# A new issue order for the first third of a two-layer state-space and local-attention kernel

## The chip, the cores and the metric

The kernel runs on one core of a Trainium2 chip. A core has a matrix engine (PE, fed by its weight loads, PEld), a vector engine (DVE), a scalar engine (ACT), a general engine (POOL) and a queue engine (SP) that issues DMAs; each takes its instructions in order from a queue of its own, and semaphores make one wait for another. The metric is the device time of one execution in microseconds. The kernel before takes 423.9 us, the median of three runs (423.18 to 425.21).

## The reference

The input u is 2048 tokens by 512 channels. Two layers follow each other, and the pair is applied twice with the same weights.

```python
x = A_u
x = x + A(layernorm(x))      # long convolution
x = x + B(layernorm(x))      # local attention, 32 heads, 8 keys at distance 0, 2, ... 14
x = x + A(layernorm(x))
x = x + B(layernorm(x))
# A: for each channel d a convolution kernel over 2048 lags l
logdA = dt * (A_re + 1j * A_im)
P = exp(logdA[:, :, None] * l)               # 512 channels x 128 modes x 2048 lags
K = einsum("dn,dnl,dn->dl", C, P, dt * B).real
y = irfft(rfft(u padded) * rfft(K padded))[:2048] + u * Dskip
```

K depends on the weights alone, so its spectrum is computed once and used by both A layers.

## The kernel before

The work falls into five stretches. From 0 to about 153 us the kernel builds the tables, the spectrum of K, the first stage of the Fourier transform of the normed input and the first convolution; the rest is attention, convolution, attention. Only the first stretch is touched.

**The order.** `KGEN` (line 353) is one string of words, and `run` (line 769) executes the words one after the other, each issuing a few instructions with a fixed engine. So the string sets the order of every engine's queue. A word may not stand ahead of the words whose results it needs; semaphores do the waiting on the chip. Where a copy can be done by two engines, the word's ending says which.

**The words.** K is handled in four quarters c = 0..3 of 128 channels.

- `q`, `m`, `l` (0 to 10) square the complex powers of exp(dt*A) eleven times: `q` squares on ACT, `m` and `l` combine on DVE; `b` copies a power to bf16 on ACT. `x0` to `x3` multiply C, dt and B on DVE, `x5` copies the result on ACT. `y` and `t` are a small copy and a load of an activation table.
- `U4:c`, `U2:c`, `U1:c`, `U256:c`, `U1024:c`, `U512:c` and `v2:c`, `v4:c`, `v8:c`, `v16..:c` extend the two tables U and V of quarter c by complex multiplication on DVE (lines 460 to 508). A name with `p` leaves the sums of products to PE: `+name` adds them by matmuls with the identity into PSUM (line 521), `=name` copies the result into the table on ACT (line 531); `0` or `1` behind the sign is the real or imaginary part. Without `p` the sums are `%name` on DVE (line 510). With `n` there are no sums, and a second table W takes the other products (line 483). `u:c`, `A:c`, `B:c` copy start columns into U and V; with `a` on ACT, else on DVE.
- `pcq` (line 558) is a product of U and V on PE, its four parts q = 0..3, in 34 matmuls, or 66 where W is used (`p00` to `p03`, `p12`, `p13`, `p20` to `p23`). `kc0` and `kc1` (line 575) copy two products each to SBUF on ACT; behind the second, four DMAs write them to DRAM (two on SP, two on POOL) and one DMA on POOL reads them back as `rows`. Since there are two tables U and two V, quarter c overwrites what quarter c - 2 has read.
- `sci` (line 593) multiplies `rows` of quarter c by a DFT matrix on PE, ten matmuls where all is done by PE (s01 to s03, s10 to s12) and five elsewhere; `oci` copies it on ACT, `eci` adds and subtracts on DVE, and the result is stored to DRAM in two DMAs on SP.
- `nj` and `Nj` (0 to 15) are statistics and application of the first layernorm, on DVE, or with `a` on ACT; `r0`, `r1`, `a0`, `a1` turn the statistics of eight rows each into scale and shift. `fj` (line 633) is the first DFT stage of row block j on PE, `zj` its copy out of PSUM, whole on ACT, or `a` and `v` for the real half on ACT and the imaginary one on DVE.
- `@Xg` words are the convolution of channel group g = 0..15: `T` transposes on PE, `t` or `a` copies (DVE or ACT), `X` second DFT stage on PE, `c` copy on ACT, `p` product with the spectrum on DVE, `v` inverse stage on PE, `V` copy on ACT (`W`: on DVE), `k` load of the spectrum for later groups by SP. Group 15 is done in halves, whose second parts are `d`, `q`, `i`, `I`. `U0` and `Y1` to `Y3` treat the last lag on DVE. After the last inverse stage PE begins the rows of y (`ps_y`, line 339).
- `w03:n` issues matmuls of n columns on PE that compute nothing used, into the PSUM tile that product or spectrum is going to take.

**PSUM.** The tiles of products and first stages (`psk`) and those of sums and spectra (`psg`) have two buffers each. A third waits until the first has been copied out.

The listing has the functions behind these words.

Of the kernel before, what the change touches and what calls it, by code (L numbers as in the profile page):

```python
# [1728 lines left out]
```

## Time and profile before

| What | us |
|---|---|
| median of three runs | 423.9 |
| lowest and highest | 423.18, 425.21 |
| the profiled execution | 424.25 |
| its span in the trace | 422.4 |
| DVE, PE, ACT busy in the span | 398.4, 379.3, 332.7 |
| POOL busy | 26.0 |
| DVE, ACT, PE busy from 0 to 160 us | 148.81, 145.33, 129.26 |

The page is one execution seen by the hardware profiler. A row of groups gives a line of the kernel, an engine, an operation with output and inputs, how often, its busy time, the mean duration of one, and the idle time of the engine ahead of it with what ended that. A row of the timeline gives the start, the time up to the end of the last merged instruction, the engine, the line and the tiles; in square brackets stands the idle time before it. One instruction's duration includes a part that overlaps with the next of its engine, so for a queue that never waits the spacing of starts is what counts. The ends of matmuls are modelled.

### The profile page before, as it was taken

How to read it: one execution, taken by the hardware profiler on the slowest of the kernel's cores; microseconds unless marked ns; L12 is line 12 of the kernel's file. 1: busy time of each engine (PE TensorE's matmuls, PEld its weight loads, DVE VectorE, ACT ScalarE, POOL GpSimd, SP SyncE). 2: the span in 40 equal slices, each digit the busy share in tenths (PEclk: the TensorE clock that was granted, in tenths of full speed). 3: DMA queues.
4: the chain of work that ended last, by engine and by line, in shares of the span. 5: the costliest groups of instructions: out<-in, count | busy, mean ns of one | idle time of the engine just before them, and what ended most of it. 6: DMA issues, size and time to landing. Idle time of an engine off the chain costs nothing.

```text
span 422.4 us, 12235 instructions
## 1 busy us (share of the span) xinstructions
PE 379.3 (90%) x5120; PEld 259.1 (61%) x5120; DVE 398.4 (94%) x730; ACT 332.7 (79%) x600; POOL 26.0 (6%) x68
## 2 busy tenths in 40 slices
PE   1157898999989999999999999889999999997996
PEld 1023585676458755587866575278855686875663
DVE  5999999999889979899999999999989999999994
ACT  6999998998979989766665699989988676663542
POOL 5000011001210000002020000000000001200000
PEclk9999999999999999999999999999999999998999
DMA  8900001254889960005480028239300009350022
GB/s 241 424 29 0 2 12 42 76 166 104 250 245 276 259 213 2 2 2 98 81 174 3 2 64 238 102 107 288 107 0 4 2 2 166 73 115 2 2 102 101
DMA packets 25822, 44.09 MB, mean 104 GB/s; under 512 B 7317, under 2 KB 17238, under 8 KB 25126
## 3 DMA queue, kind: packets, MB, share of 16 engines
q1 hardware_dynamic: 22918, 38.09, 31.9%
q0 software_dynamic: 1888, 4.56, 5.0%
q8 instruction: 40, 0.66, 0.6%
q10 hardware_dynamic: 960, 0.66, 0.5%
q14 instruction: 16, 0.13, 0.1%
HBM read 29.04 MB, written 6.95 MB: 85 GB/s over the span
## 4 chain that ended last, share of the span: by engine, by line
PE 46%; DVE 25%; ACT 7%; DMA 6%; issue 4%; SPq 2%; DVEq 0%; ACTq 0%
PE ps_qk L1207 10%; DVE prodpv L1403 9%; PE ps_v L1294 5%; DVE prodqk L1257 4%; PE vp L291 3%; PE psg L601 3%; PE Lp L1279 3%; PE po L1413 3%; PE ps_o L1443 2%; DVE Z L504 2%; DVE pab L275 2%; DMA Kt<-kt_scratch 2%; PE psk L568 2%; DMA V<-V 2%; ACT Z L1496 2%
## 5 line engine op out<-in xcount | busy, mean ns | idle before, releaser
L1403 DVE TENSOR_TENSOR prodpv<-V,Lsb 128x2048 bf16<-128x2048 bf16 x64 | 75.3, 1221 | 0.7 <-DMA V<-V 0.4
L1207 PE MATMUL ps_qk<-xnT,wqk 128*128 128x512 bf16 x256 | 59.9, 379 | 0.0
L1255 DVE TENSOR_TENSOR prodqk<-qT,N 128x1024 bf16<-128x1024 bf16 (+3 forms) x88 | 42.6, 544 | 1.9 <-ACT N L1210 1.9
L1257 DVE TENSOR_TENSOR prodqk<-qT,N 128x1024 bf16<-128x1024 bf16 (+3 forms) x56 | 40.4, 765 | 0.3 <-ACT qT L1210 0.2
L1413 PEld LDWEIGHTS <-prodpv 128*128 128x128 bf16 x1024 | 35.3, 100 | 7.2 <-DVE prodpv L1403 2.0
L275 DVE TENSOR_TENSOR pab<-xc,Kt 128x2048 bf16<-128x2048 bf16 (+1 forms) x34 | 38.8, 1154 | 0.7 <-issue 0.4
L1413 PE MATMUL po<-halves,prodpv 128*128 128x64 bf16 x1024 | 38.1, 196 | 0.9 <-DVE prodpv L1403 0.9
L1207 PEld LDWEIGHTS <-wqk 128*128 128x128 bf16 x256 | 23.7, 98 | 23.5
L269 ACT CAST xc<-xp 128x1024 bf16<-128x1024 f32 (+1 forms) x34 | 34.6, 1033 | 2.2 <-PE xp L263 1.9
L291 PEld LDWEIGHTS <-pab 128*128 128x128 bf16 x512 | 30.4, 98 | 7.0 <-DVE pab L275 3.5
L291 PE MATMUL vp<-sb_IC,pab 128*128 128x128 bf16 x512 | 33.6, 219 | 0.6 <-DVE pab L275 0.3
L1279 PEld LDWEIGHTS <-prodqk 128*128 128x128 bf16 x1024 | 29.8, 96 | 5.5 <-DVE prodqk L1257 2.5
L295 ACT CAST VT<-vp 128x1024 bf16<-128x1024 f32 (+1 forms) x31 | 32.7, 1065 | 0.6 <-PE vp L291 0.6
L1443 PE MATMUL ps_o<-wo_t,oT 128*128 128x512 bf16 x128 | 33.0, 379 | 0.0
L1279 PE MATMUL Lp<-sb_bones,prodqk 128*128 128x8 bf16 x1024 | 30.5, 166 | 1.0 <-DVE prodqk L1257 0.8
L528 PE MATMUL psadd<-Z,sb_ident 128*128 128x384 bf16 (+3 forms) x75 | 18.7, 337 | 13.1 <-DVE Z L504 7.9
L1294 PE MATMUL ps_v<-wv,xnT 128*128 128x256 bf16 x256 | 30.4, 272 | 0.0
L1424 ACT CAST oT<-po 128x512 bf16<-128x512 f32 x32 | 17.7, 589 | 13.8 <-PE po L1413 13.7
L1210 ACT CAST N<-ps_qk 128x512 bf16<-128x512 f32 x32 | 18.7, 587 | 12.1 <-PE ps_qk L1207 11.9
L1160 DVE BATCH_NORM_STATS2 ln_stats<-X 128x6 f32<-128x512 bf16 x39 | 24.9, 682 | 2.7 <-ACT X L1549 2.7
L1301 ACT CAST V<-ps_v 128x512 bf16<-128x512 f32 x32 | 18.2, 588 | 10.9 <-PE ps_v L1294 10.8
L1294 PEld LDWEIGHTS <-xnT 128*128 128x128 bf16 x256 | 24.2, 98 | 3.2
(202 smaller groups left out, 837.8 us busy)
## 6 DMA issues: line engine op xcount, KB each, us to landing
Kt<-kt_scratch SPq DMA_DIRECT2D x60, 256.0 KB, 5.5
kt_scratch<-ks SPq DMA_DIRECT2D x32, 128.0 KB, 3.0
G<-c_G SPq DMA_DIRECT2D x2, 1536.0 KB
V<-V SPq DMA_DIRECT2D x8, 288.0 KB, 7.8
X<-in_A_u_dram SPq DMA_DIRECT2D x4, 512.0 KB, 4.8
F1Tsb<-c_F1T SPq DMA_DIRECT2D x2, 1024.0 KB
V<-V SPq DMA_DIRECT2D x4, 512.0 KB
V<-V POOLq DMA_DIRECT2D x4, 384.0 KB, 8.3
```

The source lines that it names most:

```text
L269: nc.scalar.copy(xcs[cg][:, gs].rearrange("q g o l -> q (g o l)"), xps[cg][:].rearrange("q h n -> q (h n)")[:, gs.start * 128:gs.stop * 128])
L275: nc.vector.tensor_tensor(pabs[cg][:, gs], xcs[cg][:, gs].to_broadcast([128, gs.stop - gs.start, 2, 128]), kts[cg][:, gs], ALU.mult)
L291: a.last_pe = nc.tensor.matmul(vp[:, g, :], pabs[cg][:, gs.start + g, ab, :], C["IC"][:, ab, :], start=(ab == 0), stop=(ab == 1))
L295: copy(dst[..., parts(cg)[part]], vps.pop((cg, part))[:].rearrange("k g (q e) -> k q e g", e=GE))
L1207: nc.tensor.matmul(t.ps[:], wqk[:, ct, f0:f0 + 128], x_group(g)[:, :, ct], start=(ct == 0), stop=(ct == 3))
L1255: nc.vector.tensor_tensor(b.pr[:, u:u + 2 * n, 1 - halves_of[0], :], q, cols(kT[i][:, starts[0]:starts[0] + n * 128]), ALU.mult)
L1257: nc.vector.tensor_tensor(b.pr[:, u:u + 2 * n].rearrange("f u a q -> f a u q")[:, ::-1], q.unsqueeze(1).to_broadcast([128, 2, 2 * n, 64]), ...
L1279: nc.tensor.matmul(t.Lp[:, w, u % 2, u // 2, :], b.pr[:, u].rearrange("f a q -> f (a q)"), bones[:], start=False, stop=(t.parts == W // 2 ...
L1294: nc.tensor.matmul(t.ps[:, jj, :], tokens(ct, jp * 2 + jj, c), wv[:, ct, fp * 256:(fp + 1) * 256], start=(jj + ct == 0), stop=(jj == 1 and ...
L1403: nc.vector.tensor_tensor(t.p2[:, c:c + k, 0:nj, :].rearrange("p c j (d h) -> p c j d h", d=DH), m.V2[i // 2][:, c0 + c:c0 + c + k, r0:r0 ...
L1413: nc.tensor.matmul(po[jj // k][:, jj % k, c, :], t.p2[:, c - c0, jj, :], fold, start=(first and c == c0 and jj % k == 0), stop=(last and c ...
L1443: nc.tensor.matmul(t["ps"][:], m.oT[:, ft, j * 128:(j + 1) * 128], wo_t[:, ft, :], start=(start and ft == lo), stop=(ft == 3 or kept and f ...
```

## The change

The string `KGEN` is replaced by another that holds nearly the same words in another order. Some words change their engine. For the normed rows: n2 goes to ACT, n5 and n9 to DVE; N4, N11 and N12 go to ACT, N0, N5 and N15 to DVE. For the start columns: u:1 goes to ACT, B:1 to DVE. In the first DFT stage nine blocks are copied whole on ACT, five are split between ACT and DVE, and two are split with both halves on ACT; before, eight were whole and eight split. In the convolution V11 and V12 become W11 and W12 on DVE, W15 becomes V15 on ACT, and a4 with t3 take the place of a3 with t4.

The idle matmuls are written in another way: `~n` sets a number of columns, and the next PSUM tile that is taken by a sum, a product, a spectrum or a first stage gets them ahead of its own matmuls. There were 14,720 columns in twelve places, there are 8,576 in six. The words `kcm` get a variant on DVE, which the new order doesn't use.

```diff
-KGEN = ("m0 q0 b0 x1 l0 m1 q1 x0 t l1 b1 x3 x2 q2 m2 b2 l2 x5 m3 U4p:1 q3 U4:0 l3 b3 %U4:0 u:1 m4 q4 u:0 l4 b4 m5 q5 U2p:0 l5 +U2p:0 b5 "
...
-        "=0v8p:0 +U1024p:1 =1v8p:0 =U1024p:1 +U1024p:0 v8p:1 b9 +1v8p:1 w03:128 =U1024p:0 =1v8p:1 v16yn:0 +0v8p:1 w03:512 n5a U512:0 m10 "
-        "q10 %U512:0 n3a =0v8p:1 U512p:1 w03:6144 p03 n9a v16xn:0 p02 n14a +0U512p:1 +1U512p:1 v16x:1 n0a n2 =1U512p:1 l10 prep p00 n4a "
-        "k01 v16yn:1 =0U512p:1 p01 %v16x:1 v2:2 n1a U4p:2 Aa:2 %v2:2 p12 k00 c0 +U4p:2 ua:2 =U4p:2 v4p:2 Ba:2 U2:2 %U2:2 p13 +v4p:2 n6a "
-        "U256:2 k11 p10 =v4p:2 U1p:2 p11 w23:256 %U256:2 v2p:3 n7a +v2p:3 r0 =v2p:3 +U1p:2 Aa:3 v8p:2 =U1p:2 U1024:2 k10 U4:3 s01 ua:3 "
-        "%U1024:2 +1v8p:2 o01 v4:3 %U4:3 a0 =1v8p:2 +0v8p:2 %v4:3 U2p:3 n8a s03 =0v8p:2 c1 U512:2 +U2p:3 o03 =U2p:3 v16yn:2 n12a s02 "
...
-        "o10 k21 U512:3 p21 n13a %v8:3 N1a %U512:3 p20 n11a k20 v16x:3 s11 n10a %v16x:3 s13 o11 o13 p31 r1 v16y:3 N6a a1 p30 N0a %v16y:3 "
-        "k30 s00 N12 N13 f6 N8 N11 z6 p32 o00 e13 p33 N15a f1 k31 e00 z1a s23 z1v N10 f3 N14 o23 f12 N9 z3 z12v s20 z12a f11 o20 f5 e23 "
...
-        "@T12 @t12 @U0 @X10 @v8 @V7 @c10 @T13 @X11 @V8 @p10 @k15 @t13 @c11 @p11 @v9 @T14 @X12 @V9 @c12 @v10 @V10 @t14 @p12 @T15 @X13 @v11 "
-        "@c13 @X14 @V11 @t15 @c14 @p13 @p14 @v12 @V12 @X15 @c15 @d15 @p15 @q15 @v13 @v14 @v15 @i15 @Y1 @Y2 @V13 @V14 @W15 @Y3 @I15")
+KGEN = ("x0 q0 m0 l0 x2 t q1 b0 m1 l1 q2 b2 b1 x1 m2 l2 x3 q3 m3 l3 m4 x5 U4p:1 U4:0 +U4p:1 u:0 %U4:0 U2p:0 +U2p:0 b3 q4 b4 ua:1 =U4p:1 =U2p:0 "
+        "l4 v2p:0 v2:1 m5 U2p:1 U1p:0 +v2p:0 +U2p:1 q5 b5 =v2p:0 =U2p:1 l5 q6 n5 m6 l6 %v2:1 Aa:1 +U1p:0 y Aa:0 q7 =U1p:0 m7 v4p:1 l7 v4p:0 "
+        "U1p:1 b8 U256:1 b6 q8 ~2688 +v4p:1 ~1408 +v4p:0 m8 l8 b7 =v4p:0 =v4p:1 Ba:0 q9 U256p:0 ~128 +U256p:0 %U256:1 m9 B:1 l9 =U256p:0 +U1p:1 "
+        "b10 v8p:0 U1024p:1 U1024p:0 m10 =U1p:1 ~2432 +0v8p:0 n3a =0v8p:0 +1v8p:0 =1v8p:0 n9 +U1024p:0 b9 =U1024p:0 +U1024p:1 v8p:1 U512:0 q10 "
+        "=U1024p:1 l10 %U512:0 prep +0v8p:1 +1v8p:1 =0v8p:1 n14a =1v8p:1 n0a U512p:1 v16yn:0 v16xn:0 ~1152 p00 +1U512p:1 =1U512p:1 +0U512p:1 "
+        "=0U512p:1 n4a n2a n1a p03 p01 v16x:1 p02 ua:2 Aa:2 k00 v2:2 U4p:2 ~768 +U4p:2 %v2:2 %v16x:1 =U4p:2 v4p:2 U2:2 v16yn:1 %U2:2 c0 k01 s01 "
+        "o01 +v4p:2 p10 =v4p:2 n6a Ba:2 s03 n7a o03 n8a p11 p13 k10 U256:2 U1p:2 %U256:2 +U1p:2 p12 v2p:3 v8p:2 =U1p:2 +v2p:3 c1 =v2p:3 Aa:3 "
+        "ua:3 U1024:2 +0v8p:2 +1v8p:2 U4:3 %U1024:2 %U4:3 v4:3 U2p:3 k11 =0v8p:2 =1v8p:2 %v4:3 +U2p:3 s02 =U2p:3 U512:2 U256:3 %U512:2 %U256:3 "
+        "U1:3 U1024p:3 %U1:3 v16yn:2 c2 n12a s12 o02 r0 a0 Ba:3 o12 p23 +U1024p:3 n15a =U1024p:3 n13a s10 p22 s11 o10 n11a v8:3 U512:3 %v8:3 "
+        "%U512:3 v16xn:2 p20 s13 k21 N6a o11 s00 n10a r1 o13 N2a N3a o00 a1 v16x:3 v16y:3 %v16x:3 %v16y:3 N14 e13 N5 e00 N10 N8 N11a p21 p33 "
+        "N1a k20 p32 p30 p31 k31 N4a k30 N12a N7a f6 f11 z6 z11 f1 z1 s23 o23 e23 f5 z5 f3 z31a s20 o20 f8 z30v e20 z8 s21 o21 N0 f4 z4 f7 z70a "
+        "e21 s22 f14 s32 o22 z14 o32 N13 z71v f13 z13 f2 e22 z20v s33 z21a o33 e32 e33 f0 f10 z0 z100a s30 f12 o30 N9 N15 z101a z121v z120a s31 "
+        "o31 e30 f15 z150v f9 z91a z151a z90a @T0 @T1 @t0 @k4 @X0 @T2 e31 @t1 @c0 @T3 @t2 @p0 @t3 @X1 @c1 @k5 @p1 @T4 @v0 @X2 @a4 @c2 @T5 @V0 "
+        "@k6 @v1 @X3 @T6 @t5 @T7 @c3 @U0 @p2 @k7 @Y1 @p3 @X4 @V1 @v3 @c4 @X5 @v2 @k8 @V3 @c5 @V2 @t6 @p4 @t7 @T8 @p5 @t8 @X6 @c6 @v4 @V4 @k9 "
+        "@T9 @X7 @c7 @v5 @k10 @V5 @T10 @X8 @t9 @p6 @t10 @c8 @p7 @Y2 @p8 @v6 @T11 @V6 @k11 @X9 @v8 @T12 @c9 @X10 @v7 @V8 @c10 @V7 @k12 @k13 @t11 "
+        "@T13 @X11 @p9 @c11 @k14 @v9 @V9 @Y3 @t12 @T14 @X12 @p10 @v10 @c12 @V10 @t13 @T15 @p11 @t14 @t15 @p12 @X13 @c13 @p13 @v13 @V13 @k15 "
+        "@v11 @X14 @v12 @W11 @W12 @c14 @p14 @X15 @c15 @p15 @v15 @V15 @d15 @q15 @i15 @I15 @v14 @V14")
...
+        def fresh(tile):
+            warm(tile, late.pop("fill", 0))
+            return tile
...
-            ps = tiles["+", name, c, rs] = psum()[1].tile([128, 2, 512], F32, name="psadd", tag="psg")
+            ps = tiles["+", name, c, rs] = fresh(psum()[1].tile([128, 2, 512], F32, name="psadd", tag="psg"))
...
-            if part == "v":
-                nc.vector.tensor_copy(C["z_view"][:, 1, j], src[:, 1])
-            elif part == "a":
-                nc.scalar.copy(C["z_view"][:, 0, j], src[:, 0])
-            else:
+            if not part:
                 nc.scalar.copy(C["z_view"][:, :, j], src)
+                return
+            r = int(part[0])
+            (nc.scalar.copy if part[1] == "a" else nc.vector.tensor_copy)(C["z_view"][:, r, j], src[:, r])
...
-            if full[0] in "wW":
...
+            if full[0] == "~":
+                word(full, lambda full=full: late.update(fill=int(full[1:])))
```

More of the change, by code (lines that the diff above doesn't have):

```diff
@@ L508, in step, with warm @@
                 C["powers_used"] = last
+        def warm(tile, cols):
+            flat = tile[:].rearrange("n a b -> n (a b)")
+            while cols > 0:
+                n = min(cols, 512)
+                nc.tensor.matmul(flat[:, 0:n], C["ident"][:], C["ident"][:].unsqueeze(1).to_broadcast([128, n // 128, 128]), start=True, stop=True)
+                cols -= n
+        def fresh(tile):
+            warm(tile, late.pop("fill", 0))
+            return tile
         def sum_dve(name, c):
@@ L546, in spectrum_tile @@
             if ("s", c, i) not in tiles:
-                tiles["s", c, i] = psum()[1].tile([128, 2, 512], F32, name="psg", tag="psg")
+                tiles["s", c, i] = fresh(psum()[1].tile([128, 2, 512], F32, name="psg", tag="psg"))
             return tiles["s", c, i]
-        def warm(tile, cols):
-            flat = tile[:].rearrange("n a b -> n (a b)")
-            while cols > 0:
-                n = min(cols, 512)
-                nc.tensor.matmul(flat[:, 0:n], C["ident"][:], C["ident"][:].unsqueeze(1).to_broadcast([128, n // 128, 128]), start=True, stop=True)
-                cols -= n
         def product(c, q):
@@ L633, in first_stage @@
         def first_stage(j):
-            ps = tiles["f", j] = psum()[0].tile([128, 2, D], F32, name="ps_s1", tag="psk")
+            ps = tiles["f", j] = fresh(psum()[0].tile([128, 2, D], F32, name="ps_s1", tag="psk"))
             for r in range(2):
@@ L725, in kgen @@
             for m in range(2):
-                word(f"k{c}{m}", lambda c=c, m=m: product_out(c, m), f"p{c}{2 * m}", f"p{c}{2 * m + 1}", "prep")
+                for v, copy in (("", nc.scalar.copy), ("v", nc.vector.tensor_copy)):
+                    word(f"k{c}{m}{v}", lambda c=c, m=m, copy=copy: product_out(c, m, copy), f"p{c}{2 * m}", f"p{c}{2 * m + 1}", "prep")
             for i in range(4):
-                word(f"s{c}{i}", lambda c=c, i=i: spectrum(c, i), f"k{c}0", f"k{c}1")
+                word(f"s{c}{i}", lambda c=c, i=i: spectrum(c, i), *[w for w in everything if w.rstrip("v") in (f"k{c}0", f"k{c}1")])
                 word(f"o{c}{i}", lambda c=c, i=i: spectrum_odd(c, i), f"s{c}{i}")
```

9 lines of the change are left out of this document (4 added, 5 removed), and 8 rows, old and new, of the table KGEN.

## The prediction

> **What bounds the kernel now.** I read the page's busy times, then the 160 us of the changed stages (busy time, chain, waits), then the timeline of each engine there, and last the tiles and queues that a moved step touches.
>
> ```profile
> DVE  5999999999889979899999999999989999999994
> ```
> ```profile
> sum 160.00, PE 129.26 PEld 86.08 DVE 148.81 ACT 145.33 POOL 17.04; mean PE 8.08 PEld 5.38 DVE 9.30 ACT 9.08 POOL 1.06
> ```
> ```profile
> by line: PE psg L601 8.5%; DVE Z L504 6.5%; DMA Kt<-kt_scratch 6.4%; PE psk L568 6.3%; DVE pab L275 5.7%; issue 4.2%; PE psg L606 3.7%; DVE zt L254 2.5%; DVE Vsecond L483 2.2%; PE psadd L528 2.0%; DVE Vtab L483 1.9%; DMA kt_scratch<-ks 1.7%
> ```
> ```profile
> PE psadd L528 <- DVE Z L504: 8.3, 5, 6.4
> ...
> DVE Z L641 <- ACT Z L643: 2.6, 4, 1.2
> ```
>
> The first row is DVE's busy share in forty slices of the span, full from the second to the last. The sum row of the windows from 0 to 160 us: DVE works 148.8 us and ACT 145.3, so neither has room for a wait of more than a few us. The chain of these 160 us, by line, hops between all engines and the DMAs. The waits (total, places, longest) are long only on PE, which has time; DVE's longest is 2.6 us over four places. A new order has perhaps 5 us to win and everything to lose, and what counts is whether a queue gets blocked. Each engine takes its words in the written order, and that is how the timeline shows them: the products stand on PE in the list's order p03 p02 p00 p01 p12, and ACT's copies k01, k00 likewise.
>
> **The change part by part.** The anchors of the old order:
>
> ```profile
> 9.47 0.69 DVE L431 SCALAR_TENSOR_TENSOR lad<-lad 128x512 f32<-128x512 f32 x1
> ...
> 53.57 2.25 DVE L504 TENSOR_TENSOR Z<-Vtab,Z 128x1920 bf16<-128x1920 bf16 x2
> 55.71 0.72 DVE L179 BATCH_NORM_STATS2 n_stats<-X 128x6 f32<-128x512 bf16 x1
> ...
> 56.75 0.68 DVE L434 TENSOR_TENSOR L<-sq 128x512 bf16<-128x512 f32 x1
> 57.35 0.65 DVE L483 TENSOR_TENSOR Vtab<-Vtab,Z 128x960 bf16<-128x960 bf16 x1
> ...
> 61.84 0.69 DVE L663 TENSOR_TENSOR cl<-cb,L 128x1024 bf16<-128x1024 bf16 x1
> ...
> 98.80 1.38 DVE L204 TENSOR_SCALAR N<-X,n_rstd,n_nb 128x512 bf16<-128x512 bf16 x4
> ...
> 147.22 1.20 DVE L275 TENSOR_TENSOR pab<-xc,Kt 128x2048 bf16<-128x2048 bf16 x1
> ```
> ```profile
> 23.48 0.59 PE L528 MATMUL psadd<-Z,sb_ident 128*128 128x256 bf16 x2 [6.36 <-DVE Z L504]
> ...
> 24.72 1.48 PE L555 MATMUL psk<-sb_ident 128*128 128x512 bf16 x3
> 26.00 0.39 PE L528 MATMUL psadd<-Z,sb_ident 128*128 128x128 bf16 x2
> ...
> 53.40 0.50 PE L528 MATMUL psadd<-Z,sb_ident 128*128 128x512 bf16 x2
> ...
> 54.80 0.43 PE L568 MATMUL psk<-Utab,Vtab 128*64 128x40 bf16 x8
> ...
> 60.47 0.68 PE L568 MATMUL psk<-Utab,Vtab 128*64 128x40 bf16 x16
> ...
> 69.55 2.35 PE L601 MATMUL psg<-G,rows 128*128 128x512 bf16 x10
> 71.74 0.92 PE L528 MATMUL psadd<-Z,sb_ident 128*128 128x512 bf16 x4
> ...
> 96.06 0.43 PE L568 MATMUL psk<-Utab,Vtab 128*64 128x40 bf16 x8
> ...
> 98.22 1.27 PE L606 MATMUL psg<-G,rows 128*128 128x512 bf16 x5
> ...
> 119.53 0.68 PE L248 MATMUL pt<-sb_ident,Z 128*128 128x128 bf16 x9 [0.23 <-DVE Z L641]
> ...
> 152.18 0.35 PE L339 MATMUL ps_y<-VT,F1Tsb 128*128 128x448 bf16 x1
> ```
>
> A row of the timeline: start, us to its last end, engine, line, what. Costs are spacings from one start to the next. n on DVE: 55.71 to 56.75, 1.04. The two sums of U512p:1: 53.40 to 54.80, 1.4. Three products with the second table: 54.80 to 61.15, 2.1 each; two without: 96.06 to 98.22, 1.08 each. A whole spectrum: ten matmuls, 69.55 to 71.74, 2.2. v16xn:0 ended at 53.57, %v2:2 at 61.84, the tables at 98.80; the convolution's transposes began at 119.53, p13 ended at 148.4 and the rows of y began at 152.18.
>
> Step 1, p00 first. The new PE list is p00, +1U512p:1, +0U512p:1, p03, p01, p02, where the old one began with p03 p02 and both sums. p00 needs v16xn:0. DVE has more before that word: n5, n9 (2.08), l10 (0.60), B:1 (a 768-element copy, no row; between 0.2 and 0.6, I take 0.5 as a product of that width), less u:1 (0.15). So v16xn:0 ends at 53.57 + 3.03 = 56.6. p00's third and fourth blocks of matmuls need its last instruction: end 57.6. PE has had nothing to do for some 6 us since the sums of v8p:1, so its first matmuls run at half rate (three 512-column fills took 0.43 each from 24.72 to 26.00, after an idle of 6.4; the warm spacing is 0.22): I add 0.4. Then 1.4 of sums and 3 x 2.1: p02 ends at 65.75. DVE's v16x:1, v2:2, U4p:2 (2.96) are over at 59.6, and %v2:2 overwrites the table that p02 reads: done at 65.9, not 59.9. **Wait of 6.0 on DVE.** Behind the same sums ACT waits too, about as long (=1U512p:1).
>
> Step 2, s01 at once behind k01.
>
> ```profile
> 52.26 0.63 ACT L184 ACTIVATE n_junk<-X 128x512 bf16<-128x512 bf16 x1
> ...
> 53.87 0.63 ACT L184 ACTIVATE n_junk<-X 128x512 bf16<-128x512 bf16 x1
> ...
> 60.77 0.67 ACT L579 CAST KT<-psk 128x640 bf16<-128x640 f32 x1
> ...
> 62.34 0.90 ACT L697 COPY Vtab<-Z 128x768 bf16<-128x768 bf16 x1
> 63.12 0.63 ACT L184 ACTIVATE n_junk<-X 128x512 bf16<-128x512 bf16 x1
> ...
> 71.94 1.01 ACT L617 CAST ks<-psg 128x1024 bf16<-128x1024 f32 x1 [0.34 <-PE psg L601]
> 72.85 0.91 ACT L535 CAST Vtab<-psadd 128x896 bf16<-128x896 f32 x1
> ...
> 102.12 0.69 ACT L579 CAST KT<-psk 128x640 bf16<-128x640 f32 x1
> ```
> ```profile
> 66.61 0.77 POOL L590 DMA_DIRECT2D rows<-rows_scratch  x1 [3.74 <-DMA rows_scratch<-KT]
> ```
> ```profile
> 106.33 0.77 POOL L590 DMA_DIRECT2D rows<-rows_scratch  x1 [2.12 <-PE ps_s L636]
> ```
> ```profile
> DMA to landing us min/median/max: 2.7/3.0/3.2
> ```
>
> s01 reads rows that go through DRAM: after k00 and k01 there are two writes on SP, two on POOL, and a read on POOL that waits for them. In the old order the second copy ended at 61.44 and s01 began at 69.55: 8.1 us, in which PE did p12, p13, p10, p11 and three sums. The new PE queue has s01 right behind +U4p:2, and ahead of +v4p:2, p10, s03, p11, p13, +U1p:2, p12; ACT has o01 right behind k01, ahead of =v4p:2, n6a and Ba:2. After p02 ACT does ua:2 0.40, Aa:2 0.54, k00 0.58, =U4p:2 0.32, k01 0.58, with 0.1 for handing over: 68.3. Rows at 76.4 (the first trip's own 8.1; the last one took 6.5, from 102.81 to 106.33 plus the read's median of 3.0 in the last row). s01 takes 2.2 plus 1.2 for half rate after 10 us of idle: 79.8. Then o01 0.91 (71.94 to 72.85), =v4p:2 0.74, n6a 1.61 (52.26 to 53.87), Ba:2 0.78 (62.34 to 63.12): 83.9. DVE's ten words from %v16x:1 to v2p:3 are 9.6 us, done at 75.5; v8p:2 needs Ba:2. **Wait of 8.4 on DVE, about 11 on ACT.**
>
> The PE clock first by the row: half rate held for 2.5 us from 23.48, which prices s01 at +1.2. The Trainium skill, "TensorE: Matmul & The Clock Gate", Part 1, says that an idle window of about 3.4 us halves the clock and that a busy window of that length restores it; by it s01 would cost some 0.4 more and the sum would be 456. For the DRAM trip the rows say 8.1. The Trainium skill, "DMA: Bandwidth & Descriptors", on the fixed cost, gives about 2.0 us per DMA, an estimate of 4 for write and read; by that the sum would be about 451, and the trace's single read (2.7 to 3.2) does not agree.
>
> Step 3. PE's eight words behind s01, up to +v2p:3, are 10.4 us (s03 2.2, two long products 4.2, two short 2.2, three sums 1.8 by their columns at 0.22 per 512): 90.2. =v2p:3 and Aa:3 on ACT: 91.1. v4:3 needs both, and DVE is there at 87.8 (83.9, v8p:2 2.0, then 1.9). **Wait of 3.3.**
>
> Step 4. DVE from v4:3 to v16xn:2: 20.0, to 111.1. The next word is a1, which needs r1, which needs all of n8 to n15 on ACT. ACT: k11 done at 92.1, rows 6.7 later (near the last trip's 6.5), s12 to 101.0, then o12 to r1: four of n (1.61), three whole spectra copies (0.92) and four small words, 11.5 in all, and 1.2 of waits for p23 and s11: 113.8. **Wait of 2.7.** Then v16x:3, v16y:3 and their sums, 6.6: tables done at 120.5 against 98.8.
>
> Step 5, the first DFT stage. In the old order p31 and p30 ran before the tables' end; now p33 stands ahead of p32, p30, p31, all after it: 4 x 1.08, 124.9; k30 0.58: 125.5.
>
> ```profile
> L645 ACT CAST Z<-ps_s x8: 1013/1025/1082, 100.0 to 115.8; 128x1024 bf16<-128x1024 f32 x8
> L643 ACT CAST Z<-ps_s x8: 586/590/642, 102.7 to 118.0; 128x512 bf16<-128x512 f32 x8
> L641 DVE CAST Z<-ps_s x8: 680/692/692, 103.3 to 118.8; 128x512 bf16<-128x512 f32 x8
> ```
> ```profile
> L295 DVE CAST VT<-vp x3: 671/692/1218, 152.4 to 306.7; 128x512 bf16<-128x512 f32 x2, 128x1024 bf16<-128x1024 f32 x1
> ```
>
> ACT now has nine whole copies (spacing 0.93) and nine halves (0.49) where it had eight and eight; DVE five halves for eight. From k30 ACT has 18.6 of work (two N 1.4, the copies 12.8, the eight o's 4.4) plus 0.8 of waits; DVE's 16.5 and PE's 15.8 lie beside it. The transposes start at 144.9, not 119.5. Swapping which N and n each engine does is even on ACT but for one n (-1.6); it is counted in the lists above. The first Kt loads follow the rows and stores, landing some 6 us before p0: hidden, 1 for 1 if not.
>
> Step 6, the convolution up to p13 has the same DVE sum (27.8: e30 went ahead, Y1 to Y3 came in): from 119.53 to 148.4, 28.8, hence 173.7. k15 is written late, but its SP queue waits only for p10: nothing.
>
> Step 7, the tail. Old: p13's end to y 3.8. New: v13, v11, X14, v12 on PE and W11, W12 on DVE (1218 ns, spacing 1.15) before p14: p14 ends at +5.65, p15 at +6.2; q15 needs d15, which ACT has behind V15, which needs v15: +8.5; i15 and then v14 (0.9, ready long before but last in the queue): y at +10.0. That is 6.2 more: 183.7 against 152.18, **+31.5**.
>
> Fewer fills (8,576 columns for 14,720, 2.6 us of PE) free nothing, since PE waits there; missing warmth is priced above. The head's new order (x0 before m0) costs under 0.3. Everything after y is unchanged. The profiled execution took 424.25 (span 422.4), 0.35 above the median of 423.9. 424.25 + 31.5 = 455.8; against the median 455.
>
> **The rivals.**
> (a) Later slack swallows part: steps 3 and 4 cost nothing (-6.0) and step 5 stays as tight as it was (20.7, not 24.4): 446. For it: DVE's 2.6 us of waits in that stage; against: ACT's list is fuller.
> (b) A shorter DRAM trip: 6.6 instead of 8.1 and no half rate at s01: 453; with the read's minimum of 2.7 and a write as short, 452.
> (c) The clock: half rate after every PE wait, at p00, s01, s12 and p33, 1.2 more each: 460. For it: the 0.43 spacing; against: shorter idles.
> (d) Not slower: DVE alone sets the time, because PE's ends are modelled and its words may really be done well before the profile has them. The old DVE list up to the rows of y sums to 137.1 us of spacings from 9.47, the new one to 138.4 (n +1.0, B:1 for u:1 +0.35, halves of z -1.8, W11 and W12 for W15 +1.75). Back to back with 1.5 of gaps q15 then ends at 149.4, and i15 and v14 behind it let y begin at 150.9 instead of 152.18: 423.0. It decides if all waits of DVE from the tables on stay under 1.3 us. Against: step 1 alone is 6.0, and PE would have to be three products ahead of its rows.
> (e) The list isn't obeyed as written: 424. Against: the timeline obeys the old one.
>
> **How the numbers follow.** Forecast 0.52, (a) 0.18, (b) 0.10, (c) 0.15, (d) 0.04, (e) 0.01. The bounds of single terms (B:1 0.3, trip 1.5, clock 1.7, tail 3) give 448 to 460 for the likeliest; with (a) and (c), 441 to 464. Faster by over 0.5% (what the measurement can tell) is 0.02, a part of (d); same 0.03, the rest of (d) and (e); slower 0.95.
>
> **What would show it.** A DVE wait near 60 us on %v2:2 of 5 to 7, released by PE psk; an ACT wait for psg of some 10 us before o01, and one on PE for rows; a DVE wait for ACT's Vtab copy near 75; tables done near 120, transposes near 145; from the last whole pab product to y about 10 less p14's half. If PE psk or rows released none of these, the theory is wrong.

## The result and the profile after

The changed kernel takes 467.9 us (median of four runs, 467.06 to 471.1) against 424.1 for the kernel before beside it: 1.1045 times as long, 95% interval 1.0987 to 1.1103. It is 44 us slower, where 31 were forecast. The direction and most of the waits came as predicted. The sum of their prices was too low, most of all in the convolution. The profiled execution is the longest of the four (471.1, span 469.3), 3 us above the median.

Busy tenths of DVE and the granted PE clock in forty slices of the span, from the page of the changed kernel:

```profile
DVE  5999937398729797479999999999998999999994
...
PEclk9998786998879899699999999999999999999999
```

DVE's full row of 9s before the change now has holes in slices 6, 8, 12 and 17 (a slice is 11.7 us), and PE's clock is lowest in slices 5, 7, 12 and 17. What DVE waited for between 20 and 200 us (total, places, longest):

```profile
DVE Z L503 <- ACT Vtab L699: 9.2, 2, 8.2
DVE ks L633 <- ACT odd L628: 8.3, 1, 8.3
DVE Vtab L525 <- PE psk L571: 7.9, 2, 6.6
DVE n_nb L196 <- ACT n_rstd L191: 3.8, 1, 3.8
DVE pab L275 <- ACT xc L269: 3.8, 4, 2.2
DVE VT L295 <- PE vp L291: 3.8, 2, 3.1
...
DVE Z L647 <- PE ps_s L639: 0.2, 1, 0.2
```

With the rows left out the eleven add up to 44.1 us; before the change DVE's waits from 20 us to the start of y were the 2.6 that the prediction shows and 1.5 in others. The timeline rows at the prediction's steps:

```profile
9.03 1.67 DVE L852 SCALAR_TENSOR_TENSOR cb_prod<-raw_C,dt,raw_B 128x256 f32<-128x256 bf16 x4 [1.17 <-DMA raw_C<-in_A_C_im_dram]
...
56.40 0.59 PE L571 MATMUL psk<-Utab,Vtab 128*64 128x40 bf16 x8 [5.67 <-DVE Vtab L482]
...
67.50 0.27 DVE L525 TENSOR_TENSOR Vtab<-Z 128x128 bf16<-128x128 bf16 x1 [6.60 <-PE psk L571]
...
78.13 0.62 PE L604 MATMUL psg<-G,rows 128*128 128x512 bf16 x1 [8.47 <-DMA rows<-rows_scratch]
...
82.63 1.01 ACT L620 CAST ks<-psg 128x1024 bf16<-128x1024 f32 x1 [11.13 <-PE psg L604]
...
87.02 2.09 DVE L503 TENSOR_TENSOR Z<-Vtab,Z 128x1792 bf16<-128x1792 bf16 x2 [8.19 <-ACT Vtab L699]
...
120.06 0.17 DVE L196 SCALAR_TENSOR_TENSOR n_nb<-n_mv,n_rstd 128x8 f32<-128x8 f32 x1 [3.83 <-ACT n_rstd L191]
...
124.42 2.36 DVE L525 TENSOR_TENSOR Vtab<-Z 128x960 bf16<-128x960 bf16 x4
...
126.26 0.62 PE L571 MATMUL psk<-Utab,Vtab 128*64 128x40 bf16 x8 [2.67 <-DVE Vtab L525]
...
133.37 0.69 ACT L582 CAST KT<-psk 128x640 bf16<-128x640 f32 x1 [2.04 <-PE psk L571]
...
153.61 1.07 PE L248 MATMUL pt<-sb_ident,Z 128*128 128x128 bf16 x16 [1.83 <-ACT Z L647]
...
183.09 2.35 DVE L275 TENSOR_TENSOR pab<-xc,Kt 128x2048 bf16<-128x2048 bf16 x2
...
185.50 3.00 PE L291 MATMUL vp<-sb_IC,pab 128*128 128x128 bf16 x32 [2.56 <-DVE pab L275]
...
196.41 2.74 PE L291 MATMUL vp<-sb_IC,pab 128*128 128x128 bf16 x24 [1.89 <-DVE pab L275]
198.94 0.58 PE L339 MATMUL ps_y<-VT,F1Tsb 128*128 128x448 bf16 x1
```

The tables are over at 126.8 (98.8 before), k30 is copied at 134.1, the transposes start at 153.6 (119.5), p13 ends at 185.4 (148.4) and y starts at 198.9 (152.2): 46.8 later, and nothing behind y has changed. The first row is particular to this execution: x0's load came late. U4p:1 starts at 21.47 here and at 19.8 to 20.4 in the profiles of the other kernels with this head, so some 1.5 of the 46.8 is that load.

### The profile page after: what moved, and what is told of

It is laid out like the page before. It is cut to its first block, busy times and chain, and to the rows that moved or that the text cites. A ratio compares the mean times of both kernels' runs of the same rounds, so it can differ in the third digit from the quotient of the medians.

```text
span 469.3 us, 12158 instructions
## 1 busy us (share of the span) xinstructions
PE 389.8 (83%) x5063; PEld 267.0 (57%) x5107; DVE 400.0 (85%) x731; ACT 332.1 (71%) x597; POOL 25.9 (6%) x68
## 4 chain that ended last, share of the span: by engine, by line
PE 47%; DVE 31%; ACT 10%; issue 6%; DMA 4%; SPq 2%; DVEq 0%; ACTq 0%
PE ps_qk L1210 9%; DVE prodpv L1406 8%; DVE Z L503 6%; PE psk L571 6%; PE ps_v L1297 5%; PE vp L291 4%; DVE prodqk L1260 4%; PE Lp L1282 3%; PE psg L604 2%; DVE pab L275 2%; PE pt L248 2%; PE ps_o L1446 2%; PE po L1416 2%; DMA V<-V 2%; ACT Z L1499 2%
## 5 line engine op out<-in xcount | busy, mean ns | idle before, releaser
L291 PE MATMUL vp<-sb_IC,pab 128*128 128x128 bf16 x512 | 36.3, 229 | 10.3 <-DVE pab L275 9.4
L291 PEld LDWEIGHTS <-pab 128*128 128x128 bf16 x512 | 32.9, 103 | 16.3 <-DVE pab L275 12.6
L1416 PEld LDWEIGHTS <-prodpv 128*128 128x128 bf16 x1024 | 34.0, 98 | 7.9 <-DVE prodpv L1406 2.6
L1416 PE MATMUL po<-halves,prodpv 128*128 128x64 bf16 x1024 | 37.0, 193 | 1.5 <-DVE prodpv L1406 1.4
L295 ACT CAST VT<-vp 128x1024 bf16<-128x1024 f32 (+1 forms) x30 | 30.3, 1021 | 11.1 <-PE vp L291 11.1
L1446 PE MATMUL ps_o<-wo_t,oT 128*128 128x512 bf16 x123 | 32.0, 379 | 0.4
L571 PE MATMUL psk<-Utab,Vtab 128*64 128x40 bf16 x512 | 24.3, 200 | 8.9 <-DVE Vtab L482 6.3
L571 PEld LDWEIGHTS <-Vtab 128*64 128x64 bf16 x512 | 22.2, 128 | 13.5 <-issue 9.3
L503 DVE TENSOR_TENSOR Z<-Vtab,Z 128x768 bf16<-128x768 bf16 (+2 forms) x22 | 19.4, 927 | 9.2 <-ACT Vtab L699 9.2
L539 PE MATMUL psadd<-Z,sb_ident 128*128 128x512 bf16 (+3 forms) x71 | 20.7, 373 | 7.8 <-ACT Utab L549 1.8
```

The costliest lines, as they stand in the source:

```text
L291: a.last_pe = nc.tensor.matmul(vp[:, g, :], pabs[cg][:, gs.start + g, ab, :], C["IC"][:, ab, :], start=(ab == 0), stop=(ab == 1))
L503: last = nc.vector.tensor_tensor(prod[i].rearrange("n r (h e t) -> n h r (e t)", h=hn, t=2), src.rearrange("n h r e t -> n h r (e t)"), by ...
L571: nc.tensor.matmul(ps[lanes, hl, 0:2 * NU], T[:, q * 16 + hl, r].rearrange("n v t -> n (v t)"), U[c % 2][:, q * 16 + hl, r, 0:NU].rearrang ...
L1416: nc.tensor.matmul(po[jj // k][:, jj % k, c, :], t.p2[:, c - c0, jj, :], fold, start=(first and c == c0 and jj % k == 0), stop=(last and c ...
L1446: nc.tensor.matmul(t["ps"][:], m.oT[:, ft, j * 128:(j + 1) * 128], wo_t[:, ft, :], start=(start and ft == lo), stop=(ft == 3 or kept and f ...
```

## The experiments

Times are medians; ratios, with 95% intervals, are to the kernel before on the same chip. The two expectations that speak of the products of quarter 1 (e9_tables, e12_four) mean p00 to p03, which belong to quarter 0; the 14 places of fill in that of e16_no_fill are the twelve of the list.

### Step 1: which product comes first

```diff
-U512p:1 v16yn:0 v16xn:0 ~1152 p00 +1U512p:1 ... =0U512p:1 n4a n2a n1a p03 p01 v16x:1 p02
+U512p:1 v16yn:0 ~1152 p03 v16xn:0 p02 +1U512p:1 ... =0U512p:1 n4a n2a n1a p00 p01 v16x:1
```

> The changed kernel with one part of step 1 undone: PE makes p03 and p02 first, then the two sums of U512p:1, then p00 and p01, as the old list had it. Theory (a chain of blocked queues): the wait on %v2:2 (6.6 and 1.3 on DVE) and the one of ACT behind the sums (7.3) go, but both halves of KT are still needed by s01, and all four products are over only some 4 us earlier, because p03 can start 2 us before p00 could; so DVE meets the later wait at v8p:2 with 8.2 + 4 instead of 8.2, and 4 us are left of the gain: 464. Rival 1 (each wait is its own price): 7.9 less, 460. Rival 2 (what costs is the half rate of PE after its idle time, and that comes at the first product whichever it is): within 1 of 468.

Measured: 467.9, ratio 1.1057 (1.1002 to 1.1112): no gain, the number of rival 2. Three rows of its timeline:

```profile
52.68 0.59 PE L569 MATMUL psk<-Utab,Vtab 128*64 128x40 bf16 x8 [3.39 <-DVE Vtab L480]
...
64.42 0.27 DVE L523 TENSOR_TENSOR Vtab<-Z 128x128 bf16<-128x128 bf16 x1 [4.96 <-PE psk L569]
...
83.90 2.09 DVE L501 TENSOR_TENSOR Z<-Vtab,Z 128x1792 bf16<-128x1792 bf16 x2 [7.46 <-ACT Vtab L697]
```

Only 1.6 of the wait on %v2:2 has gone, because that word needs all four products and not p02 alone, and the next wait is nearly as long as it was. PE still starts at half rate (eight narrow matmuls in 0.59, 0.40 in the kernel before). I put v16yn:0 back as well:

```diff
-... v8p:1 U512:0 ... U512p:1 v16yn:0 v16xn:0 ~1152 p00 ...
+... v8p:1 v16yn:0 U512:0 ... U512p:1 ~1152 p03 v16xn:0 p02 ...
```

> The changed kernel, the products of quarter 1 in the old PE order as in the first experiment, and beside it v16yn:0 put back on DVE ahead of U512:0 and U512p:1, where the old list has it. Theory now (the first experiment failed because its four products still could not start before v16yn:0, which the change has also moved behind U512p:1 on DVE; p03 started only 2 us earlier): p03 starts some 5 us earlier, p03 and p02 and the sums are over before v16xn:0 is, the last product ends 6 to 8 us earlier, the wait on %v2:2 (5 to 6.6) is nearly gone and the rows come 6 to 8 us earlier: 460 to 462. Rival (later words take it back, as in the first experiment): 466 to 468.

Measured: 467.0, ratio 1.1005 (1.0941 to 1.1070). The theory failed again: p03 started at 52.45, held now by a column sum on DVE (%U512:0 by the order). All of DVE's queue ahead of the products is later than before (49.26), whichever word stands first. So the place of p00 in PE's queue is not what step 1 costs.

What the whole front costs was measured the other way round: the changed order up to k00 and k01, and the old one behind it.

```diff
-U2:2 v16yn:1 %U2:2 c0 k01 s01 o01 +v4p:2 p10 =v4p:2 n6a Ba:2 s03 n7a o03
+U2:2 v16yn:1 %U2:2 c0 k01 p12 Ba:2 p13 +v4p:2 n6a U256:2 k11 p10 =v4p:2
...
```

> The changed order up to k00 and k01 (head, tables of quarters 0 and 1, p00 first, one fill of each place as changed), and behind that the old order to the end, convolution and copies as before. Theory (blocked queues): k00 and k01 are copied near 69 instead of 58 and 61, everything behind them is as late as v8p:2, which starts near 76.5 instead of 68.3, and nothing later gives it back: 8 more than the kernel before, 432. Rival (the old order behind it has slack, since its rows arrive before s01 is due): 424 to 427. Rival (PE's half rate adds to it): 434 to 436.

Measured: 437.4, ratio 1.0301 (1.0273 to 1.0329): 13 us, more than the theory or either rival had.

```profile
55.23 0.59 PE L570 MATMUL psk<-Utab,Vtab 128*64 128x40 bf16 x8 [4.52 <-DVE Vtab L481]
...
71.48 0.40 PE L570 MATMUL psk<-Utab,Vtab 128*64 128x40 bf16 x8 [3.08 <-ACT Vtab L698]
...
80.03 2.09 DVE L502 TENSOR_TENSOR Z<-Vtab,Z 128x1792 bf16<-128x1792 bf16 x2 [2.46 <-ACT Vtab L548]
```

The first product is 6.0 late, v8p:2 11.8, y 12.9 (165.1 against 152.2), so nothing is given back. Some 3 of it belong to the seam, where p12 waits 3.1 for a copy that stands late on ACT. With s01 late, below, v8p:2 starts at 76.7, 8.4 later than before the change (68.3), without that seam. The front costs 8 without the seam and 13 with it.

### Step 2: s01 right behind k01

```diff
-k01 s01 o01 +v4p:2 p10 =v4p:2 n6a Ba:2 s03 n7a o03 n8a p11 p13 ... +v2p:3 c1 =v2p:3 Aa:3 ua:3 U1024:2
+k01 +v4p:2 p10 =v4p:2 n6a Ba:2 n7a n8a p11 p13 ... +v2p:3 s01 c1 =v2p:3 Aa:3 ua:3 o01 U1024:2 s03 o03
```

> The changed kernel with step 2 undone: s01, o01, s03 and o03 stand behind p10, p11, p13, p12 and the sums on PE, and behind =v4p:2, n6a, Ba:2, n7a, n8a on ACT. Theory: the waits of DVE at v8p:2 (8.2) and of ACT at o01 (11.1) go, PE does its four products in the time of the DRAM trip, and s01 runs at full rate (2.2 instead of 4.3): 8 to 11 less, 457 to 460. Rival (the trip to DRAM bounds whatever is done meanwhile, and the wait comes back at v4:3 or at the next rows): 0 to 4 less, 464 to 468.

Measured: 459.1, ratio 1.0862 (1.0807 to 1.0917), 9 less, as expected. And the part alone, in the kernel before:

```diff
-c0 +U4p:2 ua:2 =U4p:2 v4p:2 Ba:2 U2:2 %U2:2 p13 ... U4:3 s01 ua:3 ... o01
+c0 +U4p:2 ua:2 =U4p:2 s01 o01 v4p:2 Ba:2 U2:2 %U2:2 p13 ... U4:3 ua:3 ...
```

> The kernel before the change with one part of it alone: s01 and o01 right behind =U4p:2, ahead of p13, p10, p11 and the sums on PE and of Ba:2, n6a, k11 and =v4p:2 on ACT. Theory: rows land at 69.5 as before, PE stands idle for 8 us and starts s01 at half rate (some 3.4), o01 ends at 74; p11, for which %U256:2 waits on DVE, ends near 78 instead of 67, so DVE has a wait of 8 to 11 and keeps nearly all of it: 431 to 435. Rival (DVE and ACT have enough other words, and the slack before the rows of quarter 2 takes the rest): 424 to 427.

Measured: 433.9, ratio 1.0252 (1.0226 to 1.0279), 10.5 more. One row each of PE and DVE:

```profile
68.38 0.62 PE L599 MATMUL psg<-G,rows 128*128 128x512 bf16 x1 [6.03 <-DMA rows<-rows_scratch]
...
77.46 2.09 DVE L502 TENSOR_TENSOR Z<-Vtab,Z 128x1792 bf16<-128x1792 bf16 x2 [8.77 <-ACT Vtab L536]
```

The wait has the size that was forecast (8 to 11), but it came at v8p:2 and not at %U256:2; y is 8.6 later in that profile. This part costs by itself.

### Both, and the clock of PE

```diff
-U512p:1 v16yn:0 v16xn:0 ~1152 p00 +1U512p:1
+U512p:1 v16yn:0 ~1152 p03 v16xn:0 p02 +1U512p:1
...
-k01 s01 o01 +v4p:2 p10
+k01 +v4p:2 p10
```

> Both edits together. Theory: with s01 late, nothing swallows what the first edit frees, so the two are worth more than the sum of the single ones (4 and 8): 7.9 + 8.2 = 16 less, 452. Rival (independent prices): the sum of the two single gains, 456. Rival (a later wait, at r1 or the last tables, takes all back): above 460.

Measured: 462.2, ratio 1.0921 (1.0879 to 1.0963). Two undone parts are worth 3 less than one of them; the intervals overlap a little, the four times of each do not. At the transposes the two profiles are only 0.5 apart (142.9 and 143.4): up to there the first edit gains nothing, and the other 2.5 come behind. Busy time and granted clock of one stretch in which PE is at about the same part of its list, first in e2_spectrum, then in e3_both:

```profile
69.00:80.00 11.00, 9.96 (x219) 7.74 (x218) 11.00 (x27) 9.11 (x23) 1.90 (x3) 1.00 0.14 33
```
```profile
52.50:62.00 9.50, 9.50 (x153) 7.66 (x154) 6.78 (x13) 1.38 (x2) 0.00 (x0) 0.50 0.01 2
...
69.00:80.00 11.00, 11.00 (x194) 9.12 (x193) 11.00 (x28) 7.89 (x19) 1.90 (x3) 0.53 0.14 31
```

The columns are the window, its length, what PE, PEld, DVE, ACT and POOL were busy (instructions), then the granted clock, the DMA share and GB/s. In the second kernel PE runs at half rate for nearly all of 11 us in which it is never idle, and makes 194 instructions where the first makes 219 in 9.96. Whether that is the cause was tested with fills at the same order:

```diff
-~1152 p03 v16xn:0
+~8192 p03 v16xn:0
...
-k01 +v4p:2
+k01 ~3072 +v4p:2
...
-p21 p33
+p21 ~6144 p33
```

> The order of e3_both with fill matmuls in three idle times of PE: 8192 columns ahead of p03 (1152 before), 3072 ahead of +v4p:2 (none), 6144 ahead of p33 (none). Theory (PE's half rate made that run slow: 0.50 from 52.5 to 62, 0.53 from 69 to 80 and 0.50 from 115 to 124 in its profile): p03 to the sums 3 less, p10 to p12 2 to 3 less, the four products before k30 2.7 less, of which each is on the path: 454 to 456. Rival (the order itself swallows the gain): 461 to 463.

Measured: 456.0, ratio 1.0781 (1.0720 to 1.0841), 6 less, as the clock theory has it. In the profiles 3.6 of it is there at the transposes (139.8 against 143.4). The rest comes behind them, where no fill was added ("The same idle time gives two clocks", below). The same two stretches, PE being further along its list in the second:

```profile
52.50:62.00 9.50, 9.50 (x248) 7.93 (x246) 7.29 (x15) 3.90 (x10) 0.00 (x0) 1.00 0.01 2
...
69.00:80.00 11.00, 9.97 (x170) 6.99 (x168) 10.97 (x30) 7.96 (x19) 0.77 (x1) 1.00 0.08 22
```

In the changed kernel itself the same was tried ahead of p00, s01 and p33:

```diff
-~1152 p00
+~12288 p00
...
-k01 s01
+k01 ~14336 s01
...
-p21 p33
+p21 ~6144 p33
```

> The changed kernel, its order as it is, with fill matmuls that keep PE busy in three idle times: 12288 columns ahead of p00 (1152 before), 14336 ahead of s01 (none before), 6144 ahead of p33 (none before). Theory (the half rate of PE after its waits is a part of the price, and lies on the path at all three places): p00 and the sums 2.0 less, s01 2.0 less, the four products before k30 2.7 less: 6.7 less, 461. Rival (PE's clock is beside the path): within 1 of 468.

Measured: 465.0, ratio 1.0976 (1.0926 to 1.1026), 3 less and not 6.7, with intervals that overlap. Its profile has v8p:2 at 80.9, where the other kernels with this order have it at 83.8 to 85.3 (87.0 in the changed kernel's own, with its late load), so the first two places gave 3 to 4. The third gave nothing: behind it s23 met a wait of 2.8 for its rows. And the kernel before without any fill:

```diff
-U512p:1 w03:6144 p03
+U512p:1 p03
...
-p11 w23:256 %U256:2
+p11 %U256:2
```

> The kernel before without its fill matmuls (14,720 columns in 14 places). Theory (fills themselves cost nothing on the path, and without them PE makes the sums and p03 and p02 at half rate, some 2 to 4 of PE time of which the slack ahead of s01 takes a part): 1 to 3 more, 424.5 to 426.5. Rival (they only fill idle time and PE's rate there is beside the path): within 0.5 of 423.5.

Measured: 424.8, ratio 1.0011 (0.9989 to 1.0034): no difference. In its profile the second copy of KT is 2.5 later and y 1.2; the median doesn't show it.

Combining s01 late with the larger edit of step 1:

```diff
-v8p:1 U512:0
+v8p:1 v16yn:0 U512:0
...
-U512p:1 v16yn:0 v16xn:0 ~1152 p00 +1U512p:1
+U512p:1 ~1152 p03 v16xn:0 p02 +1U512p:1
...
-k01 s01 o01 +v4p:2 p10
+k01 +v4p:2 p10
```

> The edit of e9_tables and that of e2_spectrum (s01, o01, s03, o03 late) together. Theory (blocked queues, both undone): 7 + 9 = 16 less than the changed kernel, 452. Rival (PE falls into the half rate somewhere else, as in e3_both, where it held for 10 us behind an idle time of 1.7): 456 to 460.

Measured: 459.4, ratio 1.0850 (1.0817 to 1.0884), the time of s01 late alone. Its profile again has DVE wait 3.3 for sums behind s01 and s03 on PE, 0.7 longer than with s01 late alone (3.33 against 2.67).

### Step 5: behind the tables

```diff
-v16x:3 v16y:3 %v16x:3 %v16y:3 N14 e13 N5 e00 ... p21 p33 N1a k20 p32 p30 p31 k31 N4a k30
+v16x:3 %v16x:3 v16y:3 p21 p31 p30 %v16y:3 N14 e13 N5 e00 ... p32 N1a k20 p33 k30 N4a k31
```

> The changed kernel with step 5 undone: DVE sums the columns of v16x:3 before v16y:3, so that p31 and p30 run before the tables are over, and p32, p33, k30 and k31 follow. Theory: behind the tables two products are left instead of four, 7.0 of PE at half rate become 2.2 to 3.5, and the odd spectra and the transposes come 3.5 to 4.8 sooner: 463.5 to 464.5. Rival (ACT's list of copies from k30 to the transposes swallows it): within 1 of 468.

Measured: 470.1, ratio 1.1113 (1.1094 to 1.1132): no gain. The last copy of KT ended at 126.2, where it is 129.8 in e5_old_conv, whose order is the changed one up to there, and the gain went into a new wait. SP, PE and ACT in its timeline:

```profile
127.25 2.54 SPq L588 DMA_DIRECT2D rows_scratch<-KT  x4
...
133.41 2.33 PE L607 MATMUL psg<-G,rows 128*128 128x512 bf16 x5 [4.28 <-DMA rows<-rows_scratch]
...
135.82 0.59 ACT L626 COPY odd<-psg 128x512 f32<-128x512 f32 x1 [5.50 <-issue]
```

k20 had been copied at 121.5, but its write stands on SP behind the stores of e13 and e00, whose results DVE makes only after the tables. In the changed kernel such a delay (k20 copied at 124.8, s23 at 136.9) lies hidden behind the four products. Both were then undone:

```diff
-v16x:3 v16y:3 %v16x:3 %v16y:3 N14 e13 N5 e00 N10 N8 N11a p21 p33 N1a k20 ...
+v16x:3 %v16x:3 v16y:3 p21 N11a N1a k20 p31 p30 %v16y:3 N14 e13 N5 e00 N10 N8 p32 p33 k30 N4a k31
```

> The changed kernel with step 5 undone as in the run before (p31 and p30 ahead of the last two column sums), and k20 put ahead of e13 and e00, so that its two writes on SP are issued before the stores of e13 and e00. Theory now (that run gained nothing because the rows of quarter 2 waited on SP: k20 was copied at 121.5, its write was issued only at 127.3, behind the stores of e13 and e00, whose results DVE makes after the tables; s23 waited 4.3 on PE and o23 5.5 on ACT): s23 starts near 128 instead of 133.4 and the transposes some 5 us earlier, 463. Rival (ACT's list of copies up to the transposes is the bound): 467 to 470.

Measured: 464.1, ratio 1.0962 (1.0892 to 1.1032), clearly less than the run before (1.1094 to 1.1132). Against the changed kernel the intervals overlap.

```profile
120.75 1.71 SPq L588 DMA_DIRECT2D rows_scratch<-KT  x2
```
```profile
128.16 2.21 PE L607 MATMUL psg<-G,rows 128*128 128x512 bf16 x5
```

The write leaves at once, s23 starts at 128.2 and the transposes at 146.5 instead of 151.6. From v8p:2 to the transposes it takes 62.0 here and 65.4 to 67.9 in the six profiles that have both s01 and step 5 as changed. The step is worth about 4, and only if both chains are shortened.

### Steps 6 and 7: the convolution

```diff
-@T0 @T1 @t0 @k4 @X0 @T2 e31 @t1 @c0
+@T0 @k4 @T1 @t0 e31 @t1 @X0 @c0 @T2
...
-@v15 @V15 @d15 @q15 @i15 @I15 @v14 @V14
+@v13 @v14 @v15 @i15 @Y1 @Y2 @V13 @V14 @W15 @Y3 @I15
```

> The changed kernel up to the first transposes, then the convolution's words in the old kernel's order (all four odd spectra before it, as the change has them). In the profiles the stretch from the first transpose to the rows of y took 32.7 before the change and 45.3 after it (42.4 in the profile of the run with s01 moved back, where PE kept its full clock). Theory (the convolution's new order costs by itself, through copies that free their tiles late and through the chain p13, v13, W11, W12, p14, p15): the stretch comes back to 33, 10 to 12 less, 456 to 458. Rival 1 (in the convolution only PE's half rate costs, and it comes from the stalls ahead of it): 3 less, 465. Rival 2 (loads of Kt set the pace of the convolution): within 1 of 468.

Measured: 456.5, ratio 1.0785 (1.0768 to 1.0802), 11.4 less. From the first transpose to y it takes 31.9. The other direction, the changed convolution in the kernel before:

```diff
-@T0 @k4 @T1 @t0 o31 e31 @t1 @X0 @c0 @T2
+@T0 @T1 @t0 @k4 @X0 @T2 o31 e31 @t1 @c0
...
-@v13 @v14 @v15 @i15 @Y1 @Y2 @V13 @V14 @W15 @Y3 @I15
+@v15 @V15 @d15 @q15 @i15 @I15 @v14 @V14
```

> The kernel before the change up to the first transposes, and from there the changed order of the convolution and its tail (o31 and e30 stay inside the convolution, as in the old list). Nothing ahead of it stalls. Theory (the order costs by itself): 10 to 12 more than before, 434 to 436. Rival (the prediction's step 6 and 7: no cost up to p13, 6.2 in the tail): 430. Rival (only PE's half rate, brought by the earlier stalls): within 2 of 424.

Measured: 435.8, ratio 1.0307 (1.0279 to 1.0335), 12 more by the medians and 13 by the ratio. The order costs by itself.

```profile
131.97 1.01 ACT L295 CAST VT<-vp 128x1024 bf16<-128x1024 f32 x1 [1.06 <-PE vp L291]
...
142.20 1.01 ACT L295 CAST VT<-vp 128x1024 bf16<-128x1024 f32 x1 [0.96 <-PE vp L291]
```

These two waits stand ahead of V3 and V8, whose products come last.

```diff
-@v3 @c4 @X5 @v2 @k8 @V3 @c5 @V2 ... @v8 @T12 @c9 @X10 @v7 @V8 @c10 @V7
+@v2 @c4 @X5 @v3 @k8 @V2 @c5 @V3 ... @v7 @T12 @c9 @X10 @v8 @V7 @c10 @V8
```

> The run e7_new_conv (the kernel before, with the changed order of the convolution) with two pairs put in rising order: v2, v3, V2, V3 instead of v3, v2, V3, V2, and v7, v8, V7, V8 instead of v8, v7, V8, V7. Theory (ACT waits for the later product first: 1.06 and 0.96 in that run's profile, and PE 1.15 and 1.05 for the same products): 2 to 3 less than that run, 433. Rival (the waits belong to DVE's products p2 and p3 or p7 and p8 and only change places): within 1 of 435.8.

Measured: 434.8, ratio 1.0235 (1.0208 to 1.0261) against 1.0307 for the run it starts from. Both waits are gone. From the transposes to the end of p13 it takes 29.8 instead of 31.9, and the tail behind it 13.1 instead of 13.4. So some 2 of the 13 is the reversed pairs (1 by the medians, 3 by the ratios), which falls between the two forecasts, and most of the rest is in the tail.

### The head, and four parts at once

```diff
-x0 q0 m0 l0 x2 t
+m0 q0 l0 x0 x2 t
```

> The changed kernel with x0 put behind m0 and l0, so that DVE makes the ladder's first products while the load that x0 needs is still under way. Theory (the head costs because DVE waits for that load ahead of everything: U4p:1 starts at 20.0 in most profiles of the changed kernel, at 21.5 in one and at 18.4 to 19.0 in the kernels with the old head): U4p:1 at 18.6, 1.4 less, 466.5. Rival (the prediction: under 0.3): 468.

Measured: 468.9, ratio 1.1043 (1.1004 to 1.1082): nothing, and U4p:1 still starts at 19.6, where the old head has it at 18.4 to 19.0. So the wait for that load is not what makes the head late, the changed kernel's own profile apart.

The edits of e9_tables, e2_spectrum, e10_rows and e5_old_conv together:

```diff
-U512p:1 v16yn:0 v16xn:0 ~1152 p00 +1U512p:1
+U512p:1 ~1152 p03 v16xn:0 p02 +1U512p:1
...
-k01 s01 o01 +v4p:2 p10
+k01 +v4p:2 p10
...
-N11a p21 p33 N1a k20 p32 p30 p31 k31
+p21 N11a N1a k20 p31 p30 %v16y:3 N14 e13
...
-@T0 @T1 @t0 @k4 @X0 @T2 e31 @t1 @c0
+@T0 @k4 @T1 @t0 e31 @t1 @X0 @c0 @T2
```

> The changed kernel with four parts undone at once: the tables and products of quarter 1, s01 and s03 late, the end of the tables with k20 ahead of e13, and the old convolution order; the head, the order of the words of quarters 2 and 3, and the copies split as changed stay. Theory (these four are the causes, worth 7 + 9 + 5 + 11.5): 435. Rival (they overlap, each swallowing a part of another): 440 to 448. Rival (nothing else in the change costs): 424 to 428.

Measured: 442.9, ratio 1.0455 (1.0414 to 1.0497). The four are worth 25, not 33, and 19 remain. Of these the front, as e13_front prices it, can account for 8 to 13, since the edits of step 1 in e12_four did not undo it: its profile still has DVE waits of 3.6 and 1.2 at %v2:2. The remaining 6 to 11 were not taken apart. They may lie in the words of quarters 2 and 3 and in the first DFT stage, where the same profile has DVE waits of 3.3 for sums, 2.9 at a1 (step 4) and 4.2 for the odd spectra.

## What the prediction had right, and the steps that failed

**Mechanism.** Right: in-order queues are blocked by a word that is put ahead of its time, DVE stops being full, and nothing later gives it back. Rival (d), DVE back to back, needed all waits from the tables on under 1.3 us; DVE waited 44. Rival (a) fell too: step 5 cost more, not less.

**The steps that failed** are 6 and 7. From the transposes to y they have 38.8 (28.8 and 10.0); the profile shows 45.3. That is 6.5 of the 15.2 by which y comes later in the profile (198.9) than in the sum (183.7). Of the rest 3.1 is there at v8p:2 (87.0, not 83.9; 1.5 of it is the late load), 3.2 more at a1 (120.1, not 113.8), and step 5 adds 2.4.

**Step 6** put the convolution up to p13 at nothing because DVE's sum was equal. It took 31.8 and not 28.8: the reversed pairs V3, V2 and V8, V7 hold up PE and ACT, some 2. **Step 7**, the tail, was forecast at 6.2 more and took 9.7 more (13.5 against 3.8). It was summed with PE at full rate. Behind p13, PE's half rate makes v13, the last v's and the start of y longer (3.00 for two v's against 1.96 at full rate), which the sum left out. In e2_spectrum, where these two v's ran at full rate, the tail took 11.3, so about 2 of the 3.5 is that burst. The last v's were not tried with fills. The changed convolution costs 12 to 13 by itself, in a kernel that has no stall ahead of it, and 11.4 in the changed one.

**Step 1** named the right wait (6.0 forecast, 6.6 and 1.3 measured) and the wrong cause. It is not p00's place and not p02: %v2:2 waits for all four products, and these are late because DVE's words ahead are. Taking a part of the wait away changed nothing that can be measured. How late it makes the rest was nearly right: the sum has DVE ready for v8p:2 at 75.5 without step 2, and with s01 late it starts at 76.7. The head, put at under 0.3, starts U4p:1 some 1 to 2 later (19.8 to 20.4 against 18.4 to 19.0). Mis-sized in step 1: PE's half rate, 0.4 forecast for p00. In the profile p00 and the sums take 5.9 (56.4 to 62.3), where 2.1, 0.4 and 1.4 make 3.9.

**Step 2** came out right in size: 8.4 forecast, 8.2 measured for DVE, 11 and 11.1 for ACT, and 9 to 10.5 of time. That was partly luck, since two errors cancelled. The trip through DRAM took 6.6 (71.5 to 78.1), as in rival (b), and s01 took 4.3 instead of 3.4, towards rival (c).

**Steps 3 and 4**, 3.3 and 2.7, came at 3.7 and 3.8 (2.9 in the other profiles). Step 3 was right only in its sum: it is four waits of 0.7 to 1.1, and only one of them is the one forecast, of v4:3 for ACT's copy. In step 4 ACT waited 3.9 between o12 and r1 (2.24, 0.94 and 0.70, all for PE), where the sum has 1.2.

**Step 5** failed in two ways. The four products took 7.0 and not 4.3, all at half rate; ACT's list from k30 to the transposes was right (19.5 against 19.4). And of k20, which is moved too, its writes on SP were not followed past the stores of e13 and e00; "hidden" was said of the Kt loads only. When the place of the products alone is undone, that queue holds the transposes where they are, as e6_last and e10_rows show.

**The fills** "free nothing": right, 1.0011 without any. "Warmth is priced above": wrong in size. Filling gave some 3 in the changed order and 6 in e3_both (3.6 by the transposes), so rival (c), 1.2 at each of four places, pointed the right way, but was itself too small and without the tail. The Trainium skill, "TensorE: Matmul & The Clock Gate", Part 1, was weighed at s01 as 0.4 more than the sum had; 0.9 was measured.

The single prices, 8 to 13 for the front, 9 to 10.5 for s01, 4 for step 5 and 11 to 13 for the convolution, make 32 to 41 of the 44. They are not independent, so the rest isn't a clean remainder.
